# Squared-ReLU attention and a maxout layer on one core: a fourth query step by seven products, with z of the second sequence turned earlier

## The chip, the core and the metric

The kernel runs on one core of a Trainium2 chip. Its engines work side by side: TensorE (PE in the profile, PEld its weight loads) multiplies, VectorE (DVE) and ScalarE (ACT) do the elementwise work, GpSimd (POOL) and SyncE (SP) issue transfers. The metric is the device time of one execution in microseconds. Three runs of the kernel before gave 937.58, 938.73 and 940.17 us: median 938.73.

## The reference

For each of 8 sequences of 3072 rows, with z of 64 columns and u and v of 256:

```
scores = (z @ z.T) / 3072
attn   = maximum(scores, 0) ** 2
x      = u * (attn @ v)                 # 24576 rows of 256
out    = maximum(x @ w1, x @ w2) @ w_out    # 1024 hidden columns
```

The attention matrix is symmetric, so a block that one step has computed can be transposed for a later one. The kernel uses max(x@w1, x@w2) = relu(x@(w1-w2)) + x@w2, so that x@w2@w_out becomes x@(w2@w_out), with w2@w_out (W2o) computed once.

## The kernel before, in words

**Steps.** A step n is one sequence b and 512 of its queries (s = 0 to 5): 48 steps. Its 3072 keys are 24 blocks of 128, in 6 groups of four. A *pair* (n, k0) is two key blocks against 512 queries. Its scores are two matmuls that fill one PSUM tile of the pool `mm` (three tiles for the whole kernel), a relu on ACT or DVE takes them to an `a_sb` tile in SBUF, and a square follows there. Steps 0 to 3 compute all 12 pairs themselves. From step 4 on a step takes most groups from earlier steps by DMA transposes (`aT`, issued on SP) and computes fewer pairs, its diagonal group among them.

**Product with v.** A *plain* step (n < PLAIN, here steps 0 to 3) multiplies 24 blocks by two halves of v: 48 matmuls of 512 columns. The other steps use a scheme of the Strassen kind: each group takes 14 matmuls of 256 columns (six X, eight Y) in place of what would be eight of 512. X of all groups comes first, then Y. In exchange DVE folds v (four subtractions per group and sequence, one of them in place, after the last plain read of that group), adds blocks of the attention tiles (`es`, three or four additions per group of 128x512; four `es` tiles), and puts the result together (`e`, `t`) before it is scaled by u to `xT`.

**Second part.** d(n), 16 matmuls with w1-w2 in four jobs, a relu each to `g_sb`; o(n), 40 matmuls with w_out and W2o in two jobs, two copies to `o_sb` and a store. They lag: a non-plain step n does o(n-3), then X, d(n-2), Y. Before, plain step 3 has d(0), W2o with o(0), and d(1) laid among its products, each after six more key blocks. W2o needs w_out loaded and w2 loaded and turned (`w2T_sb`).

**What sets the order.** The order on PE is written out by a planner (lines 888 to 1033). It lists the work without scores, with planned times (`begins`). Scores are put in by *windows* of three pairs (the first three windows have two), in order of step and key. Going backwards from the last window, each is put at the latest allowed spot that is not later than when its first reader needs it less a latency (6.5 us for a step's own pairs, or 2.592 us where n <= 3 is plain), and not later than the next window's spot less a gap (2.1 us for early windows, 2.4 us later). A spot is not allowed inside d, o or W2o (`shared`), nor within 0.86 us behind or 1.7 us ahead of one, and in steps before step 3 only every 2.592 us from the step's start (`apart`). I call these early spots *slots*: four in each of steps 0, 1 and 2, slot 0 to slot 11. A window for which no spot is left goes to the very start of the list:

```python
found = [i for i in spots if begins[i] <= limit]
i = found[-1] if found else 0
laid.setdefault(i, []).insert(0, w)
limit = begins[i] - (GAP if w > n_first else GAP_FIRST)
```

Windows 0 and 1 are done in a hand-written head, and window 2 is always put behind the first two product jobs (lines 1019 and 1020). By the rule, window 14 (pairs 6, 8, 10 of step 3) has slot 11, each window before it one slot less, and window 3 (pairs 12, 14, 16 of step 0) slot 0; windows 15 to 18 stand within step 3.

All other engines follow a list scheduler (lines 1279 to 1332): with a cost for each job it repeatedly takes, over all engines, the job that can start first, and among those that can start at the same moment the one that is due first. DVE leaves a relu to ACT where ACT would end it sooner. The result is a fixed program order on each engine.

**Loads and turns.** `at_step(b, s, us)` names the first PE job at or behind that planned time after the start of a step. The load of z for sequence 1 (POOL, into `z_sb`) comes at step 3 plus 5 us, its two turns into `zT` (SP, DMA transposes) at step 4 plus 4 us; w_out is loaded at step 2 plus 9 us. The first score window of sequence 1 (window 19) stands early in Y of step 4.

Of the kernel before, what the change touches and what calls it, by code (L numbers as in the profile page):

```python
# [11 lines left out]
def kernel(  # L12
# [36 lines left out]
    LAG = 3  # L49
    NDIR = 3  # L50
    NDIAG = 3
    PLAIN = 4
    NA, NT = 12, 12
    scale = 1.0 / S
    c2 = float(scale * scale)
# [30 lines left out]
    def load(timed=False, **kw):  # L86
        dma = pin(nc.gpsimd.dma_start(**kw))
        if timed:
            tc.add_manual_dep(
                dma.ins,  # L90
                newest[0].name,
                mybir.DependencyInfo(mybir.DependencyClass.Sync, mybir.DependencyReason.DATA),
                reason="timed load",
            )
# [40 lines left out]
    w_out_sb = consts.tile([P, KF, D], bf16)  # L135
# [39 lines left out]
    def job(key, ways, fn, deps=(), new=None, uses=(), after=(), lag=100):  # L175
        assert key not in jobs, key
        jobs[key] = Job(key, ways, fn, deps, new, uses, after, lag)
# [5 lines left out]
    def tile_of(pool, key):  # L183
        return bufs[pool, key].tile

    class Step:
        def __init__(self, n, b, s):
            self.n, self.b, self.s, self.q = n, b, s, seqs[b]
            self.plain = n < PLAIN
            self.count = [0] * KD  # L190
# [74 lines left out]
    def add_v(b, g, at):  # L265
        buf("v", (b, g), lambda: vpool.tile([P, G, D], bf16, name="v_sb"))

        def fetch(_):
            load(
                timed=at is not None,  # L270
                out=tile_of("v", (b, g)),
                in_=v[b].rearrange("(p t) d -> p t d", p=P)[:, ds(g * G, G), :],
            )

        job(("v", b, g), {"POOL": 1300}, fetch, new=("v", (b, g)), after=at or (), lag=8000)
# [184 lines left out]
    def add_sums(st, g):  # L460
        n = st.n
        es = ("es", (n, g))
        buf("es", (n, g), lambda: spool.tile([P, 3, GW], bf16, name="es"))
        if g in st.early:
            src = ("T", (st.b, g, st.s))
            i = NG * st.b + g
            ready = [("turn", i, k0) for k0 in (G * st.s, G * st.s + 2)]
        elif g == st.s:
            src = ("A", (n, g))
            ready = [("square", n, None), ("square", n, -1), ("turn", n, None, 0), ("turn", n, None, 1)]  # L470
        else:
            src = ("A", (n, g))
            ready = [("square", n, k0) for k0 in (G * g, G * g + 2)]
# [417 lines left out]
    def put(ns, shares, key, reads=()):  # L891
        work.append((ns, shares, key, reads))

    def put_d(n):
        if n >= 0:
            for i in range(KF // 2):
                put(864, True, ("d", n, i))

    def put_o(n, per=2):
        if n >= 0:  # L900
            for i in range(G // per):
                put(1090 * per, True, ("o", n, i))

    def rows_read(st, g):
        if g in st.early:
            return [((NG * st.b + g, k0), LAT_TURNED) for k0 in (G * st.s, G * st.s + 2)]
        if g == st.s:
            return [((st.n, None), LAT_DIAG)]
        return [((st.n, k0), LAT_OWN) for k0 in (G * g, G * g + 2)]

# [3 lines left out]

    for n, st in enumerate(steps):
        if not st.plain:
            put_o(n - LAG)
            for which in range(2):
                if which:
                    put_d(n - LAG + 1)  # L920
                for g in st.groups:
                    for m in range(G // 2):
                        put(
                            PE256 * (4 if which else 3),
                            False,
                            ("XY"[which], n, g, m),
                            rows_read(st, g) if not which else (),
                        )
            continue
        within = {}  # L930
        lat = LAT_OWN if n > LAG else 6 * 432
        if n == LAG:
            within = {
                3: lambda: put_d(0),
                6: lambda: (put(1800, True, ("w2o",)), put_o(0)),
                9: lambda: put_d(1),
            }
        own = st.rows
        n_plain = 0

        def put_plain(ks, dcs, reads):
            global_i = len(plain_todo)
            i = sum(t[0] is st for t in plain_todo)
            plain_todo.append((st, i, ks, dcs))
            put(PE512 * len(ks) * len(dcs), False, ("plain", st.n, i), reads)

        for i, k0 in enumerate(own):
            if i in within:
                within[i]()
            if i in ((0, 1) if n else ()) + (len(own) - 2, len(own) - 1):  # L950
                if i in (0, len(own) - 2):
                    ks = [own[i], own[i] + 1, own[i + 1], own[i + 1] + 1]
                    for dc in range(KD):
                        put_plain(ks, [dc], [((n, own[i]), lat), ((n, own[i + 1]), lat)])
                continue
            for k in (k0, k0 + 1):
                put_plain([k], range(KD), [((n, k0), lat)])
# [38 lines left out]

    for n in range(PLAIN, len(steps)):
        i = first_of[n]
# [13 lines left out]
    for w in reversed(range(len(windows))):  # L1012
        limit = min([limit] + [due[r] for r in windows[w] if r in due])
        found = [i for i in spots if begins[i] <= limit]
        i = found[-1] if found else 0
# [24 lines left out]
    def at_step(b, s, us):  # L1040
        return pe_job_at(starts[NG * b + s] + us * 1000)
# [32 lines left out]
    def add_z(b, at, turn_at):  # L1074
        def fetch(_):
            load(
                timed=True,
                out=z_sb_0[:, 1 : 1 + NSB, :],
                in_=z[b].rearrange("(p t) d -> p t d", p=P),
            )  # L1080

        def turn_z(_):
            seqs[b].zT = make_zT(z_sb_0)

        job(("z", b), {"POOL": 1800}, fetch, after=at, lag=7500)
        job(("zT", b), {"SP": 3500}, turn_z, deps=[("z", b)], after=turn_at, lag=3500)
# [9 lines left out]
            add_u(n, at_step(pb, ps, 2 if pb == 0 else 4))  # L1096
    for b in range(1, B):
        if b == 1:
            z_at, zT_at = (3, 5), (4, 4)
            v_at = [(4, 8), (4, 14), (5, 1), (5, 4), (5, 9.5), (5, 11)]  # L1100
        else:
            z_at, zT_at = (2, 9), (3, 12)
            v_at = [(3, 8), (4, 2), (4, 8), (4, 13), (5, 9.5), (5, 11)]
        add_z(b, at_step(b - 1, *z_at), at_step(b - 1, *zT_at))
        for g, at in zip([1, 2, 3, 4, 5, 0], v_at):
            add_v(b, g, at_step(b - 1, *at))
# [4 lines left out]
    for tile_sb, source, key, at, new, rows in (  # L1111
        (lambda: tile_of(*W2), moe_w2, "w2", (0, 7), W2, "(c p) f -> p c f"),
        (lambda: w1_sb, moe_w1, "w1", (1, 3), None, "(c p) f -> p c f"),
        (lambda: w_out_sb, moe_w_out, "wo", (2, 9), None, "(c p) d -> p c d"),
    ):

        def fetch(_, tile_sb=tile_sb, source=source, rows=rows):
            load(timed=True, out=tile_sb(), in_=source.rearrange(rows, p=P))

        job((key,), {"POOL": 2000}, fetch, new=new, after=at_step(0, *at), lag=6500)  # L1120
# [57 lines left out]
    for args in plain_todo:  # L1178
        st, i, ks, dcs = args
# [4 lines left out]
    for st in steps:  # L1184
        if not st.plain:
            for g in st.groups:
                add_sums(st, g)
        add_ends(st)
# [231 lines left out]
```

## Time and profile before

| | us |
|---|---|
| median of three runs | 938.73 (937.58 to 940.17) |
| the profiled execution, its own time | 938.97 |
| its span, first to last instruction | 937.2 |
| PE busy | 927.7 (99%) |
| DVE busy | 763.2 (81%) |
| ACT busy | 688.4 (73%) |
| POOL busy | 58.6 (6%) |

The span lies 1.77 us below the execution's time. The granted clock of TensorE is 1.00 over the whole span. In the timeline a line is a run of like instructions on one engine: start, duration, line of the code, operation, tiles, shape, count, and in brackets the idle time ahead of it with what ended it. Nearly all matmuls are recorded at line 80, a helper, and so the tile names tell them apart: `s_ps<-zT` are scores, `acc<-...` products with v, `s_ps<-xT,w_sb` is d, `s_ps<-w_out_sb,...` and `s_ps<-W2o_sb,xT` are o. L219 and L221 are relus on ACT and DVE, L225 and L227 squares. Recorded durations of matmuls overlap; the chain's lines give the pace.

### The profile page before, as it was taken

To read this page: it belongs to the slowest core of one execution; us is meant where nothing else is said; L and a number is where in the kernel's file an instruction comes from. 1 tells how busy PE (TensorE), PEld (TensorE's weight loads), DVE (VectorE), ACT (ScalarE), POOL (GpSimd) and SP (SyncE) were. 2 spreads that over 40 slices of the span, in tenths; PEclk is the share of its full clock that TensorE was granted. 3 is DMA by queue.
4 is the path that set the end of the run, shared out by engine and by line. 5 is a ranking of instruction groups with operands and counts; after the bars stand their busy time and mean duration, and the time that the engine had idled before them with its cause. 6 is when DMAs were issued, how large, how long until landed. Compare 5 with 4: busy or idle time off the path is not lost.

```text
span 937.2 us, 18895 instructions
## 1 busy us (share of the span) xinstructions
PE 927.7 (99%) x7318; PEld 667.4 (71%) x7326; DVE 763.2 (81%) x1890; ACT 688.4 (73%) x829; POOL 58.6 (6%) x115
## 2 busy tenths in 40 slices
PE   8999999999999999999999999999999999999998
PEld 3355677777777777777777777777767777777786
DVE  6963898878987889778897888888888887988751
ACT  7876786579856797677877778876787658885634
POOL 2000100000000000000000000000100000000000
PEclk9999999999999999999999999999999999999999
DMA  8996998998989888899998978998899798987611
GB/s 140 168 171 111 168 167 154 156 166 136 180 149 167 146 145 162 171 163 144 142 166 173 162 136 142 188 153 160 145 164 163 148 149 169 150 166 133 124 47 68
DMA packets 365866, 140.84 MB, mean 150 GB/s; under 512 B 344272, under 2 KB 345936, under 8 KB 365776
## 3 DMA queue, kind: packets, MB, share of 16 engines
q1 hardware_dynamic: 349216, 109.89, 62.9%
q0 software_dynamic: 16560, 29.74, 21.8%
q8 instruction: 57, 0.93, 0.4%
q14 instruction: 33, 0.27, 0.1%
HBM read 59.77 MB, written 25.17 MB: 91 GB/s over the span
## 4 chain that ended last, share of the span: by engine, by line
PE 96%; ACT 2%; DMA 1%; SPq 1%; DVE 0%; issue 0%
PE s_ps L80 48%; PE acc L80 48%; DMA zT<-z_sb 1%; ACT a_sb L219 1%; SPq L83 1%; ACT g_sb L219 0%; ACT a_sb L225 0%; DMA o_sb<-in_z_dram 0%; PE tpz L109 0%; DVE a_sb L221 0%; ACT zT L110 0%; DVE a_sb L227 0%; DVE xT L240 0%; ACT o_sb L230 0%; DVE z_sb L154 0%
## 5 line engine op out<-in xcount | busy, mean ns | idle before, releaser
L80 PEld LDWEIGHTS <-v_sb 128*128 128x128 bf16 x2304 | 223.8, 98 | 83.8 <-issue 38.0
L219 ACT ACTIVATE a_sb<-s_ps 128x1024 bf16<-128x1024 f32 (+1 forms) x236 | 217.1, 975 | 35.8 <-PE s_ps L80 33.0
L225 ACT ACTIVATE a_sb<-a_sb 128x1024 bf16<-128x1024 bf16 (+1 forms) x224 | 218.5, 1013 | 0.1
L80 PE MATMUL s_ps<-w_out_sb,g_sb 128*128 128x256 bf16 x1504 | 194.9, 273 | 0.0
L80 PE MATMUL acc<-es,v_sb 128*128 128x256 bf16 x844 | 192.9, 274 | 0.0
L219 ACT ACTIVATE g_sb<-s_ps 128x1024 bf16<-128x1024 f32 x181 | 170.8, 1028 | 12.2 <-PE s_ps L80 12.2
L80 PE MATMUL s_ps<-xT,w_sb 128*128 128x512 bf16 x768 | 173.4, 379 | 0.0
L80 PEld LDWEIGHTS <-lf 128*128 128x128 bf16 x1584 | 155.0, 98 | 21.6
L233 DVE TENSOR_TENSOR es<-a_sb 128x512 bf16<-128x512 bf16 x300 | 119.8, 422 | 59.8 <-PE acc L80 59.6
L80 PE MATMUL acc<-es,lf 128*128 128x256 bf16 x740 | 167.1, 273 | 0.0
L80 PE MATMUL acc<-a_sb,lf 128*128 128x256 bf16 x600 | 163.5, 273 | 0.0
L80 PEld LDWEIGHTS <-g_sb 128*128 128x128 bf16 x1504 | 147.1, 98 | 17.5
L80 PE MATMUL acc<-a_sb,v_sb 128*128 128x256 bf16 (+1 forms) x784 | 150.6, 298 | 0.9 <-issue 0.5
L221 DVE TENSOR_SCALAR a_sb<-s_ps 128x1024 bf16<-128x1024 f32 (+1 forms) x112 | 127.5, 1140 | 21.3 <-PE s_ps L80 20.9
L80 PE MATMUL acc<-aT,v_sb 128*128 128x256 bf16 x668 | 139.7, 273 | 0.0
L80 PEld LDWEIGHTS <-w_sb 128*128 128x128 bf16 x768 | 75.2, 98 | 81.0
L230 ACT COPY e<-acc 128x512 f32<-128x512 f32 x88 | 52.1, 592 | 105.5 <-PE acc L80 105.2
L230 ACT COPY o_sb<-s_ps 128x512 f32<-128x512 f32 (+1 forms) x92 | 53.2, 578 | 87.8 <-PE s_ps L80 87.8
L80 PE MATMUL s_ps<-zT 64*128 64x512 bf16 (+1 forms) x696 | 94.8, 366 | 4.0 <-DMA zT<-z_sb 2.9
L227 DVE TENSOR_TENSOR a_sb<-a_sb 128x1024 bf16<-128x1024 bf16 (+1 forms) x124 | 79.6, 652 | 0.1
L80 PE MATMUL s_ps<-W2o_sb,xT 128*128 128x256 bf16 x384 | 73.3, 273 | 0.0
L80 PE MATMUL acc<-aT,lf 128*128 128x256 bf16 x244 | 66.5, 273 | 0.0
(53 smaller groups left out, 701.9 us busy)
## 6 DMA issues: line engine op xcount, KB each, us to landing
out_dram<-o_sb SPq DMA_DIRECT2D x47, 512.0 KB, 3.8
v_sb<-in_v_dram POOLq DMA_DIRECT2D x48, 256.0 KB, 4.9
u_sb<-in_u_dram POOLq DMA_DIRECT2D x48, 256.0 KB, 5.3
aT<-a_sb SPq DMA_TRANSPOSE x228, 4.1
z_sb<-in_z_dram POOLq DMA_DIRECT2D x7, 384.0 KB, 5.2
a_sb<-a_sb SPq DMA_TRANSPOSE x88, 2.6
w_sb<-in_moe_w_dram POOLq DMA_DIRECT2D x2, 512.0 KB, 7.7
uT<-u_sb SPq DMA_TRANSPOSE x48, 3.3
```

The lines of the kernel that those rows point to most:

```text
L80: newest[0] = pin(nc.tensor.matmul(*args, **kw)).ins
L83: pin(nc.sync.dma_start(**kw))
L219: pin(nc.scalar.activation(out_ap, in_ap, AF.Relu))
L221: pin(nc.vector.tensor_single_scalar(out=out_ap, in_=in_ap, scalar=0.0, op=ALU.max))
L225: pin(nc.scalar.activation(ap, ap, AF.Square))
L227: pin(nc.vector.tensor_mul(ap, ap, ap))
L230: pin(nc.scalar.copy(out_ap, in_ap) if eng == "ACT" else nc.vector.tensor_copy(out_ap, in_ap))
L233: pin(nc.vector.tensor_add(*args))
```

## The change

Step 3 becomes a step of the seven-product scheme (PLAIN goes from 4 to 3). It still computes all 12 pairs itself, so that its groups are 0 to 5, all taken from its own tiles; the condition for the diagonal group asks for `st.diag` now, which step 3 does not have. Its order on PE is d(0), W2o, o(0), X, d(1), Y. Its pairs are due by the rule of the other non-plain steps (6.5 us ahead of X). The load of w_out moves to step 2 plus 2 us, that of z for sequence 1 to step 2 plus 11 us, and its turn to step 3 plus 8 us.

```diff
-    PLAIN = 4
+    PLAIN = 3
...
-        elif g == st.s:
+        elif st.diag and g == st.s:
             src = ("A", (n, g))
...
     def rows_read(st, g):
...
-        if g == st.s:
+        if st.diag and g == st.s:
             return [((st.n, None), LAT_DIAG)]
         return [((st.n, k0), LAT_OWN) for k0 in (G * g, G * g + 2)]
...
         if not st.plain:
+            if n == LAG:
+                put_d(0)
+                put(1800, True, ("w2o",))
             put_o(n - LAG)
...
-        within = {}
         lat = LAT_OWN if n > LAG else 6 * 432
-        if n == LAG:
-            within = {
-                3: lambda: put_d(0),
-                6: lambda: (put(1800, True, ("w2o",)), put_o(0)),
-                9: lambda: put_d(1),
-            }
...
         for i, k0 in enumerate(own):
-            if i in within:
-                within[i]()
...
-            z_at, zT_at = (3, 5), (4, 4)
+            z_at, zT_at = (2, 11), (3, 8)
...
-        (lambda: w_out_sb, moe_w_out, "wo", (2, 9), None, "(c p) d -> p c d"),
+        (lambda: w_out_sb, moe_w_out, "wo", (2, 2), None, "(c p) d -> p c d"),
```

`add_sums`, `add_ends` and the planner are unchanged otherwise; they now serve step 3 as they serve steps 4 to 47.

## The prediction

> **What bounds the kernel now.** I read the page's busy times first, then the chain that ended last, then who waited for whom, and then the timeline of the first 100 us, where the change lies. The page's first part:
>
> ```profile
> span 937.2 us, 18895 instructions
> PE 927.7 (99%) x7318; PEld 667.4 (71%) x7326; DVE 763.2 (81%) x1890; ACT 688.4 (73%) x829; POOL 58.6 (6%) x115
> ```
>
> PE is busy for all but 9.5 us, so a change can gain only by less PE work or by removing one of PE's few waits. The list of waits (total, times, longest) has one large one on PE:
>
> ```profile
> PE s_ps L80 <- DMA zT<-z_sb: 2.9, 1, 2.9
> ```
>
> The chain shows what it hangs on, two turns of z for sequence 1, and the pace of the work around it (start, length, count):
>
> ```profile
> 57.14 3.45 PE s_ps L80 x16
> ...
> 60.60 0.86 PE acc L80 x4
> ...
> 64.09 6.11 PE s_ps L80 x56
> ...
> 87.77 8.18 DMA zT<-z_sb
> ...
> 145.36 3.93 PE acc L80 x36
> ```
>
> The pace: d takes 3.45 us, W2o with o(0) 6.11, a plain product 0.86/4 = 0.215, a product of 256 columns 3.93/36 = 0.109. The wait itself in PE's timeline, and PE's start, where the change will also act:
>
> ```profile
> 10.12 0.61 PE L80 MATMUL s_ps<-zT 64*128 64x512 bf16 x4 [0.32 <-DVE zT L110]
> 11.23 0.39 PE L80 MATMUL s_ps<-zT 64*128 64x512 bf16 x2 [0.51 <-ACT a_sb L219]
> 11.79 0.81 PE L80 MATMUL acc<-a_sb,v_sb 128*128 128x512 bf16 x3 [0.16 <-issue]
> ...
> 15.39 0.82 PE L80 MATMUL s_ps<-zT 64*128 64x512 bf16 x6
> 16.15 2.76 PE L80 MATMUL acc<-a_sb,v_sb 128*128 128x512 bf16 x12
> ...
> 95.99 0.71 PE L80 MATMUL s_ps<-zT 64*128 64x512 bf16 x6 [2.87 <-DMA zT<-z_sb]
> ```
>
> Window 3 at 10.12 and 11.23 (slot 0), its third pair waiting for a relu to free PSUM; window 4 at 15.39 (slot 1), the next one is at 18.84 and so on, 3.45 us from slot to slot, of which 0.76 are the window (15.39 to 16.15). ACT and DVE at the start:
>
> ```profile
> 11.22 1.06 ACT L225 ACTIVATE a_sb<-a_sb 128x1024 bf16<-128x1024 bf16 x1
> 12.18 1.00 ACT L219 ACTIVATE a_sb<-s_ps 128x1024 bf16<-128x1024 f32 x1
> 13.08 1.05 ACT L225 ACTIVATE a_sb<-a_sb 128x1024 bf16<-128x1024 bf16 x1
> 14.03 1.01 ACT L219 ACTIVATE a_sb<-s_ps 128x1024 bf16<-128x1024 f32 x1
> ...
> 11.18 2.35 DVE L221 TENSOR_SCALAR a_sb<-s_ps 128x1024 bf16<-128x1024 f32 x2
> 13.45 0.68 DVE L227 TENSOR_TENSOR a_sb<-a_sb 128x1024 bf16<-128x1024 bf16 x1
> 14.05 1.22 DVE L221 TENSOR_SCALAR a_sb<-s_ps 128x1024 bf16<-128x1024 f32 x1
> ```
>
> Both run without a pause: a relu every 0.90 us on ACT and 1.15 on DVE, squares 0.95 and 0.60.
>
> **Seven products in step 3.** Out: 48 x 0.215 = 10.32 us. In: 84 x 0.109 = 9.16. **Gain 1.16**, all on PE. DVE gets 24 additions, back to back 0.34 each (DVE's timeline has five of them from 98.56 to 99.90), 8.2 us, plus seven small operations and four scalings of 0.42 for two of 0.69; ACT two copies of 0.59. From 60 to 90 us DVE is busy only 3.07, 5.18 and 2.42 of each 10 us, so I cost them at nothing; without that cover the last two groups' sums (2.7 us), which wait for an `es` tile until Y has begun, would stop PE. Steps 4 and 5 lose one addition each.
>
> **z turned earlier.** The load now issues in d(0), about as early as before (then 61.13), but the turns come behind o(0) instead of after o(1), some 19 us sooner (67.4 for 86.42, by the sum below). With 8.2 us to land they are there about 17 us ahead of window 19. **Gain 2.87.** Next late at that place: nothing, the `mm` tiles are free and later windows ran unhindered. On SP the two turns take 4.66 us; queued behind them are the store of o(0), turns of step 3 (first read in X of step 4) and of its diagonal. The load of z passes that of u(4) on POOL (0.53 us of issue), which nobody needs for 20 us. w_out issues at about 47 for 53.71 on POOL; its landing took 7.0, and W2o asks for it at 61.
>
> **Small waits around step 3.** Products at 50.87 and 62.42 start 0.16 us late each, and the first ones of step 3 wait 0.07 for xT(2) at 53.46. Behind step 2 now comes d(0), which needs neither. Between 0 and 0.4, I take a **gain of 0.3**.
>
> **o(0) directly behind W2o and d(0).** Four relus of d(0) ended 4.83 us after d(0) began (56.98 to 61.81); o(0) will ask for them at 3.45 + 1.75 = 5.2. A square in ACT's way costs up to 0.95, less the 0.4 of slack. Between 0 and 0.6; I take a **loss of 0.2**.
>
> **The score windows.** This is the part that the diff does not show. X of step 3 reads its first pairs 9.6 planned us after the step's start, one group each 0.65 us, so with the 6.5 us of latency all four windows of step 3 are due between 3.1 and 5.7 us into it: inside d(0), W2o and o(0), where no spot is. Window 16 falls back to slot 11, and so every earlier one moves two slots forward: window 5 gets slot 0, and windows 4 and 3 find none and go to the start of the list with it. So nine pairs, not three, are scored ahead of the first product, through three PSUM tiles. Walking the scheduler's rule by hand (a square that can start goes before a relu that becomes ready 0.2 us later; the same walk on the old order gives the rows above), ACT does square, relu, square, relu, relu, square, relu; DVE relu, relu, square, relu, relu, square, relu. With the pitches above the relus free PSUM at 12.4, 13.1, 13.5 (window 3) and 15.0, 15.3, 15.9 (window 4), so the last pair of window 5 is scored at 16.0 and the first product starts at 16.3 instead of 11.8. Window 2 then waits for a relu until 17.9, eight products follow, and slot 1 comes at 19.95 instead of 15.39: 4.56 later. Two windows of 0.76 have been done ahead, and are missing in step 3 later: **loss 4.56 - 1.52 = 3.04**. Lower bound: all relus ahead of all squares gives slot 1 at 18.5, a loss of 1.5. Upper: one more square of 0.95 on each engine in the way, 5. The walk is nearest to the rows, so I take 3.04. After it, slots of 3.45 us follow as before: three relus and squares take 2.8 us of ACT and 2.4 of DVE.
>
> **Sum.** -1.16 - 2.87 - 0.3 + 0.2 + 3.04 = -1.1 us on the profiled execution's 938.97, which stands 0.24 over the median: 937.6 against 938.73. With all bounds: 935.8 to 940.3.
>
> **Rivals.** *The start costs little* (relus first, or the squares' place in the order kinder): loss 0 to 1.4, time 934.6 to 936.0. For it: ACT and DVE have 3 us of squares to spare there. Against it: the rule by which the old order comes out right.
>
> *The clock falls at the start.* At 1.19 six matmuls of 512 columns take 2.74 us, 0.45 each, and full pace is only there after 7: 5.5 us at half speed. If the thin scores between 10 and 16 us brought that back, it would cost 2 to 2.7 us: 939.6 to 940.3. Against it: behind the 2.87 us of waiting the next 24 products took 2.73, full pace. [...]
>
> *W2o waits for the turned w2* (the slower end). Before, its turn was issued at 45.03 and landed 6.1 us later, with W2o at 63.93: slack of 9 to 13 us. By the sum, the issue comes at about 49.5 to 52 (its trigger is 4.56 later, behind turns of 2 us each in a DMA stretch with a share of 1.08), landing 55.6 to 58, and W2o stands at 57.9 + 3.45 = 61.3. Should the queue hold it beyond 61.3, each us is one on PE, in order; from 65.4 on the kernel is over 0.3% slower, 941.6 to 943.6. For it: four turns took 10.77 us on SP at 57.79. Against it: slack is still 3 us.
>
> **Numbers.** Three tenths of a per cent, 2.8 us, is about what measuring this kernel tells from no change: 935.9 to 941.5 is "same". Forecast 0.56, cheap start 0.22, clock 0.10, w2 0.12. Faster: 0.22 and the forecast's lower edge, 0.03. Slower: 0.12 and 0.02 for edges. The range 934.9 to 941.2 leaves out the w2 case and the cheapest starts, under 2 in 10.
>
> **What would show it.** First product near 16.3 and slot 1 near 20.0; pairs of `s_ps<-zT` at 12 to 16 us each waiting on relus. No wait on `zT`; turns of z at 67 to 76. Step 3's part: d, W2o, o, 36 products, d, 48 products without a pause, and o(1) near 81.6 (before 80.33). Wrong would be: a first product by 13, a wait ahead of W2o or Y, or matmuls of 512 columns at 0.45 after 10 us.

## The result, and the profile after

Over 18 runs each, the changed kernel takes 940.47 us (median, 938.21 to 943.68), the kernel before 938.00 (935.50 to 940.17). The ratio is 1.0026 [1.0015, 1.0037]: slower by 2.4 us, between 1.4 and 3.5. The forecast was 1.1 us faster, so its sign was wrong and it stands 3.5 us off, though the time lies inside its range and within the 0.3% that it called no change.

The profiled execution of the changed kernel took 939.5 us. The page's first part:

```profile
span 937.7 us, 19013 instructions
PE 929.6 (99%) x7362; PEld 671.2 (72%) x7362; DVE 770.6 (82%) x1919; ACT 689.8 (74%) x833; POOL 58.4 (6%) x115
```

PE has 1.9 us more busy time than before (929.6 against 927.7), although 48 matmuls of 512 columns have been traded for 84 of 256, which was to save 1.16. In all PE waits less than before (8.1 us of the span against 9.5); some matmuls last longer. PE's timeline shows which:

```profile
9.33 0.61 PE L80 MATMUL s_ps<-zT 64*128 64x512 bf16 x4 [0.32 <-DVE zT L110]
10.45 0.39 PE L80 MATMUL s_ps<-zT 64*128 64x512 bf16 x2 [0.51 <-ACT a_sb L219]
11.66 0.61 PE L80 MATMUL s_ps<-zT 64*128 64x512 bf16 x2 [0.83 <-DVE a_sb L221]
12.45 1.03 PE L80 MATMUL s_ps<-zT 64*128 64x512 bf16 x4 [0.17 <-ACT a_sb L219]
14.30 1.52 PE L80 MATMUL s_ps<-zT 64*128 64x512 bf16 x6 [0.82 <-ACT a_sb L219]
15.76 1.89 PE L80 MATMUL acc<-a_sb,v_sb 128*128 128x512 bf16 x4
...
20.35 0.82 PE L80 MATMUL s_ps<-zT 64*128 64x512 bf16 x6
```

Four products of 512 columns last 1.89 us at 15.76, where four took 1.03 before (at 60.43); two scores take 0.61 at 11.66 and 0.39 at 10.45. I read the same stretch in windows of 3.41 us, half of the 6.83 us that the clock stays at 1.00 and then at 0.50 in this trace (columns: the window, its length, PE busy with the count of matmuls, granted clock, DMA share, GB/s):

```profile
4.78:8.19 3.41, 3.41 (x34) 1.00 1.10 170
8.19:11.61 3.42, 1.82 (x10) 1.00 1.12 202
11.61:15.02 3.41, 2.36 (x10) 0.50 0.94 175
15.02:18.43 3.41, 3.41 (x12) 0.50 0.31 61
18.43:21.84 3.41, 3.41 (x20) 1.00 1.00 190
```

The clock stands at half from 11.61 to 18.43 us. Before, the stretch from 9.73 to 13.14 had PE busy for 2.20 of 3.41 us and the clock at 1.00. Later in the same timeline:

```profile
58.21 3.62 PE L80 MATMUL s_ps<-xT,w_sb 128*128 128x512 bf16 x16
61.66 1.91 PE L80 MATMUL s_ps<-w_out_sb,w2T_sb 128*128 128x256 bf16 x16
...
81.59 0.27 PE L80 MATMUL acc<-es,v_sb 128*128 128x256 bf16 x1 [0.40 <-DVE es L233]
...
95.18 0.86 PE L80 MATMUL s_ps<-zT 64*128 64x512 bf16 x6
```

The 2.87 us of waiting for z at window 19 are gone. W2o follows d(0) without a pause. One new wait has come, 0.40 us for an `es` tile near the end of Y of step 3.

To set executions side by side I measure from window 3 (9.33 here, 10.12 before), because the stretch ahead of it takes 9.2 to 10.3 us in the 14 profiles. From there slot 1 comes after 11.02 us (before 5.27), and d(3) after 101.03 (before 100.91).

### The profile page after: what moved, and what is told of

Same layout as the page of the kernel before. It is cut to its first block, busy times and chain, and to the rows that moved or that the text cites. A ratio compares the mean times of both kernels' runs of the same rounds, so it can differ in the third digit from the quotient of the medians.

```text
span 937.7 us, 19013 instructions
## 1 busy us (share of the span) xinstructions
PE 929.6 (99%) x7362; PEld 671.2 (72%) x7362; DVE 770.6 (82%) x1919; ACT 689.8 (74%) x833; POOL 58.4 (6%) x115
## 4 chain that ended last, share of the span: by engine, by line
PE 96%; DMA 1%; DVE 1%; ACT 1%; SPq 0%; issue 0%; DVEq 0%
PE s_ps L80 48%; PE acc L80 48%; DMA uT<-u_sb 1%; ACT a_sb L219 0%; DVE es L233 0%; DMA o_sb<-in_z_dram 0%; ACT a_sb L225 0%; SPq L83 0%; PE tpz L109 0%; DVE a_sb L221 0%; DVE a_sb L233 0%; ACT zT L110 0%; ACT o_sb L230 0%; DVE lf L236 0%; DVE a_sb L227 0%
## 5 line engine op out<-in xcount | busy, mean ns | idle before, releaser
L80 PE MATMUL acc<-es,v_sb 128*128 128x256 bf16 x864 | 197.8, 274 | 1.0 <-DVE es L233 0.9
L80 PEld LDWEIGHTS <-lf 128*128 128x128 bf16 x1620 | 158.5, 98 | 23.7 <-issue 1.1
L233 DVE TENSOR_TENSOR es<-a_sb 128x512 bf16<-128x512 bf16 x312 | 125.3, 425 | 60.7 <-PE acc L80 60.7
L80 PE MATMUL acc<-es,lf 128*128 128x256 bf16 x756 | 170.8, 273 | 0.0
L80 PE MATMUL acc<-a_sb,lf 128*128 128x256 bf16 x624 | 170.1, 273 | 0.0
L80 PE MATMUL acc<-a_sb,v_sb 128*128 128x256 bf16 (+1 forms) x768 | 144.9, 294 | 0.0
L233 DVE TENSOR_TENSOR a_sb<-a_sb 128x512 bf16<-128x512 bf16 x156 | 66.3, 426 | 1.1
```

Of the source, the lines that this page charges most:

```text
L80: newest[0] = pin(nc.tensor.matmul(*args, **kw)).ins
L233: pin(nc.vector.tensor_add(*args))
```

## The experiments

The theory after the result: the start costs the 3.04 us of waits that the prediction worked out, and on top of it the clock falls; step 3 and z bring what was forecast. The main rival: the clock only shows up beside the loss, and the loss is the waits alone, or a wait in step 3.

In the table, "slot 1" and "d(3)" are counted from window 3 in the profiled execution; slot 1 is left out where the slots lie otherwise. Ratios are to the kernel before, run beside each.

| kernel | median us (runs) | ratio | slot 1 | d(3) |
|---|---|---|---|---|
| before | 938.00 (18) | 1 | 5.27 | 100.91 |
| after | 940.47 (18) | 1.0026 [1.0015, 1.0037] | 11.02 | 101.03 |
| blank products at the start | 938.71 (12) | 1.0008 [0.9994, 1.0021] | 9.90 | 101.62 |
| z alone | 936.15 (12) | 0.9975 [0.9963, 0.9988] | 5.27 | 98.12 |
| z alone, again | 936.71 (12) | 0.9978 [0.9965, 0.9991] | 5.27 | 98.12 |
| windows alone | 943.25 (6) | 1.0049 [1.0031, 1.0068] | 11.13 | 104.13 |
| without the z move | 945.83 (5) | 1.0082 [1.0065, 1.0098] | 11.28 | 107.22 |
| six pairs ahead | 938.43 (12) | 1.0014 [0.9989, 1.0039] | | 99.76 |
| relus first | 946.49 (6) | 1.0071 [1.0048, 1.0095] | 10.29 | 108.00 |
| windows spread | 936.64 (12) | 0.9974 [0.9960, 0.9988] | | 97.93 |
| windows spread, again | 936.74 (12) | 0.9990 [0.9967, 1.0012] | | 97.41 |
| spread, two waits taken out | 936.96 (12) | 0.9975 [0.9961, 0.9988] | | 96.85 |
| w_out earlier | 938.55 (1) | | 11.05 | 101.06 |
| spread, w_out earlier | 936.92 (12) | 0.9982 [0.9964, 1.0000] | | 97.40 |

### Blank products at the start

The changed kernel; PE gets products of a blank tile behind each of the first nine score pairs, so that it is busy while it waits for PSUM. Nothing reads them.

```diff
             for j in range(2):
                 score(q, s_tile(key)[:, j, :], j, k0 + j, st.s, 0, G)
+            if ("score", n, k0) in front:
+                idle((0, 2, 3, 2, 0, 4, 0, 1, 0)[front.index(("score", n, k0))])
...
+    front = pe_order[: pe_order.index(("plain", 0, 0))]
```

> The changed kernel with 13 products of a blank tile (512 columns, result discarded) put between the first nine score pairs on PE, so that TensorE is not thin between 10 and 16 us; nothing else changes. Theory F (the front: nine pairs ahead of the first product cost PE 3.0 us of waits, and the fall of the granted clock to 0.5 from 11.6 to 18.4 us costs another 1.2 to 1.7): the clock stays at 1.00 from about 5 us on, slot 1 comes about 1.2 us sooner than in the changed kernel (20.35), time 938.7 to 939.4. Rival L (the front is made up for later, and the loss sits in the later program, in waits for the sums and for u): the clock may stay, the time does not move: 940.2 to 940.8.

The windows of this kernel at the same place, and its W2o:

```profile
9.73:13.14 3.41, 3.05 (x15) 1.00 1.11 205
13.14:16.56 3.42, 3.27 (x18) 1.00 0.43 80
```

```profile
62.65 1.92 PE L80 MATMUL s_ps<-w_out_sb,w2T_sb 128*128 128x256 bf16 x16 [1.25 <-ACT g_sb L219]
```

With PE busy for 3.05 and 3.27 us of these windows the clock stays at 1.00, and slot 1 comes 9.90 us after window 3. The prediction's walk had 9.83 at full clock. So the waits were sized right, and the fall costs 11.02 - 9.90 = 1.1 us at this place. In the medians the two kernels differ by 0.0018, 1.7 us, with intervals that would also take 0.1 or 3. The profiled execution gives its gain back at W2o, which waits 1.25 us. The view names ACT for it, but the relus of d(0) were through: the weight loads of `w2T_sb` stood 1.7 us for the DMA of that tile, which landed 12.5 us after its issue, at 62.6. So the clock is not all that the forecast missed: with it held, the kernel stands 0.75 us over the kernel before by the medians (between 0.6 under and 2.0 over), where 1.1 under was forecast.

### z alone

The kernel before with only the load and turn of z moved.

```diff
-            z_at, zT_at = (3, 5), (4, 4)
+            z_at, zT_at = (2, 11), (3, 8)
```

> The kernel before with only z of sequence 1 loaded at step 2 plus 11 us and turned at step 3 plus 8 us; step 3 stays plain. Theory F: the 2.87 us of waiting ahead of the first window of sequence 1 go, nothing else moves: 2.9 us below the kernel before, about 935.1. Rival L (another wait takes its place, in later steps): 0 to 1 us below, 937 to 938.

Window 19 in PE's timeline, with no wait:

```profile
96.01 0.82 PE L80 MATMUL s_ps<-zT 64*128 64x512 bf16 x6
```

From window 3 to d(3) it gains 100.91 - 98.12 = 2.79 us, the wait almost to the last. The medians give 2.35 [1.1, 3.5] here and, in a second series, 2.06 [0.8, 3.3]; 2.87 lies within both.

> The kernel of the run named z_only once more (plain step 3, z early): 2.1 to 2.4 us under the kernel before, as measured. Both theories.

### Windows alone

The kernel before, with its product of step 3 as it was, but windows 3 to 16 put where the changed kernel has them.

```diff
+    at_of = {w: i for i, ws in laid.items() for w in ws}
+    slots = [at_of[w] for w in range(3, 15)]
+    laid = {i: [w for w in ws if w > 16 or w < 3] for i, ws in laid.items()}
+    for w in range(16, 2, -1):
+        laid.setdefault(slots[max(w - 5, 0)], []).insert(0, w)
```

> The kernel before (step 3 plain, z where it was) with windows 3 to 16 put where the changed kernel has them: window 16 at slot 11, each earlier one a slot less, and windows 3, 4 and 5 at the very start. Theory F: 3.0 us of waits on PE in the first 20 us and the fall of the clock (1.2 to 1.7 us), less 0.3 for the two windows that no longer interrupt step 3; the wait for zT stays 2.9: about 4 us over the kernel before, 941.5 to 942.5. Rival L: under 1.5 us over it, below 939.5.

It is 0.49% slower, the loss without the gains, and 0.75 us above its expectation. Slot 1 comes 11.13 us after window 3, and the clock is at half from 12.12 to 18.95. At d(3) it is 3.22 us behind the kernel before; its wait for z was 1.79 instead of 2.87, so that the start cost 3.22 + 1.08 = 4.3 us. That is the 3.04 of the prediction and 1.2 of clock. Step 3 of this kernel has no seven-product scheme, so the loss comes from the windows and not from step 3's arithmetic.

### Without the z move

The changed kernel with z loaded and turned where it was before.

```diff
-            z_at, zT_at = (2, 11), (3, 8)
+            z_at, zT_at = (3, 5), (4, 4)
```

> The changed kernel with z loaded and turned where it was before (step 3 plus 5 us, step 4 plus 4 us). Theory F: the wait for zT ahead of window 19 is back, 2 to 2.9 us: 942.5 to 943.3, 4.5 to 5.3 over the kernel before. Rival L (the wait was hidden or is replaced): 940 to 941.5.

It came out over both expectations. PE's wait for z, and the windows around it:

```profile
99.36 1.25 PE L80 MATMUL s_ps<-zT 64*128 64x512 bf16 x6 [3.37 <-DMA zT<-z_sb]
```

```profile
94.64:98.05 3.41, 1.35 (x11) 1.00 1.00 135
98.05:101.47 3.42, 2.11 (x11) 0.50 0.96 282
101.47:104.88 3.41, 3.41 (x18) 0.50 0.11 24
```

Behind the wait of 3.37 us the clock is at half a second time, from 98.05 to 104.88. In the changed kernel the stretch from d(2) to d(3) is 19.60 us, here 25.53: 3.37 of the difference is the wait, and 2.56 is left for the matmuls at half clock behind it.

This is what misled the prediction. In the profiled execution before, the wait of 2.87 us fell across two windows, with PE busy for 1.47 and 2.49 us, and the clock stayed at 1.00:

```profile
91.65:95.06 3.41, 1.47 (x11) 1.00 1.05 251
95.06:98.48 3.42, 2.49 (x23) 1.00 0.86 126
```

Other executions of the kernel before had a lower clock: of 92 beside the experiments, 17 show a mean clock of 0.998 or less, and in the largest series the five at 0.998 have a median of 940.40 against 938.14 of those at 1.00. Of 24 runs with z alone, none is below 0.999. That the wait for z is what takes the clock down in those 17 is argued from this, not seen: the one profile of the kernel before has no fall.

### Six pairs ahead

The changed kernel with slots every 2.16 planned us instead of 2.592, so that two more windows find one, and six pairs instead of nine are scored ahead of the first product.

```diff
-        return n >= LAG or (at - starts[n]) % (6 * 432) == 0
+        return n >= LAG or (at - starts[n]) % (5 * 432) == 0
```

> The changed kernel with early windows allowed each 2.16 us of a step (five slots a step): one window more than before stands at the front (six pairs ahead of the first product), not two. Theory F: waits at the front cost 1.2 us instead of 3.0; the granted clock either holds (936.9) or falls as with nine pairs (938.7). Rival P: no gain over the changed kernel, 940 or more.

```profile
10.43:13.85 3.42, 1.70 (x12) 1.00 1.11 205
13.85:17.26 3.41, 3.08 (x10) 0.50 0.15 28
```

Here the clock is at half for one window of 3.41 us, 13.85 to 17.26, where the changed kernel has two; PE was busy for 3.08 us of it, and full pace followed. The median fits the expectation with a fall (938.7), but by itself it decides little: the six runs at 0.998 have a median of 938.15, the three at 1.00 of 937.86, and two runs of 946.75 and 949.53 widen the interval.

### Relus first

The changed kernel, with the squares of the first nine pairs held behind the last of their relus: the prediction's lower bound for the start.

```diff
+    front = pe_order[: pe_order.index(("plain", 0, 0))]
...
+    for key in front:
+        jobs[("square",) + key[1:]].after.append(("relu",) + front[-1][1:])
```

> The changed kernel with the squares of the first nine pairs held behind the last of their relus, so that ACT and DVE free PSUM first; nine pairs still stand ahead of the first product. Theory F: front waits 1.5 us instead of 3.0, slot 1 about 1.5 us sooner; with the clock falling as before 939.0, with the clock holding 937.3. Rival (the squares are needed as soon, and PE waits for them ahead of its first products of step 0 instead): 940 to 941.

Later, on DVE and on PE:

```profile
48.59 1.29 DVE L240 SCALAR_TENSOR_TENSOR xT<-acc,uT 128x512 bf16<-128x512 f32 x2 [5.17 <-DMA uT<-u_sb]
49.34 1.01 PE L80 MATMUL acc<-a_sb,v_sb 128*128 128x512 bf16 x2 [4.86 <-DVE xT L240]
```

It missed. Slot 1 comes 10.29 us after window 3, sooner than 11.02 and with one window of half clock (14.13 to 17.55). But a later product waits 4.86 us until DVE has done `xT`, and DVE had itself waited 5.17 us for u's turn. The clock falls again from 48.27 to 55.09. Why that turn came so late is not shown. The kernel says nothing on the cheap start, only that its price can't be had by this edit.

### Windows spread

The changed kernel with a spot allowed every 0.432 planned us in steps 0 to 2. The gap of 2.1 then sets the distance: 14 windows stand 2.16 planned us apart, and two pairs are scored ahead of the first product.

```diff
-        return n >= LAG or (at - starts[n]) % (6 * 432) == 0
+        return n >= LAG or (at - starts[n]) % 432 == 0
...
-    laid.setdefault(spots[0] + 2, []).insert(0, 2)
+    laid.setdefault(spots[0], []).insert(0, 2)
```

> The changed kernel, but the planner may put early score windows at any key block (not only each 2.592 us) and window 2 goes ahead of the first products: the 14 windows ahead of d(0) then stand every 2.16 planned us, two pairs are scored ahead of the first product and not nine, all four windows of step 3 stay ahead of d(0). Theory F (front waits 3.0, clock 1.8): both go, the clock stays at 1.00; what is left is z (2.1 to 2.9), the products (1.2) and small waits (0.3) as gains, sums and W2o (0.4 to 1) as losses: 934.5 to 935.7, about 3 under the kernel before. Rival P (pace: ACT and DVE cannot take three pairs in 2.9 us, so that the waits for relus only move into the slots of steps 0 to 2): 937 or more.

The pile at the start is gone, the clock is at least 0.999 in all 12 runs, and the kernel is faster than before by 0.26% [0.12, 0.40]. Against the changed kernel that is 0.0052, 4.9 us. It fell about 1 us short of its expectation. Two waits in step 3 were in its way, one for the `es` tile, the other at W2o:

```profile
58.75 1.92 PE L80 MATMUL s_ps<-w_out_sb,w2T_sb 128*128 128x256 bf16 x16 [0.47 <-DMA w2T_sb<-w_sb]
```

### Spread, with the two waits taken out

On top of it, w2 is turned one step sooner, and three relus that stood on DVE among the last sums of step 3 go to ACT.

```diff
-        after=at_step(0, 2, 2),
+        after=at_step(0, 1, 6),
...
+    for key in (("relu", 4, 22), ("relu", 5, None), ("relu", 5, -1)):
+        jobs[key].ways = {"ACT": jobs[key].ways["ACT"]}
```

> The kernel of the run named spread (seven products, z early, windows every 2.16 us) with the turn of w2 at step 1 plus 6 us instead of step 2 plus 2, and the three relus of window 18 left to ACT. Theory W (what the seven products save in step 3, 1.2 us, goes to two new waits there: 0.47 us and more ahead of W2o, 0.4 to 0.56 us for the last sums in Y): both waits go from the profile and the time is about 1 us under that of spread. Rival (the gain is lost elsewhere, in the windows' closer pace or in later sequences): the waits go, the time stays within 0.4 us of spread.

> The kernel of the run named spread once more, beside spread_fix and z_only2 on one chip: 2.3 us under the kernel before, as measured. Theory W: it stands level with z_only2 within 0.5 us, since its 1.2 us of saved products are spent on the two waits in step 3. Rival (the seven products are a gain by themselves once the front is mended): 1 us under z_only2.

Both waits went from step 3. The second series of the spread kernel has two runs with a lower mean clock (940.87 at 0.998, 945.31 at 0.995), which widen its interval; its other ten have a median of 936.03. The profiled executions of this kernel and of z alone (second series) have window 3 at 10.26 and 10.27. d(3) of this kernel and of z alone:

```profile
107.11 3.62 PE L80 MATMUL s_ps<-xT,w_sb 128*128 128x512 bf16 x16
```

```profile
108.39 3.62 PE L80 MATMUL s_ps<-xT,w_sb 128*128 128x512 bf16 x16
```

This kernel is ahead by 1.28 us, where the trade of products was to give 1.16. The medians do not show it: 936.96, 936.74 and 936.71 for this kernel, the spread one and z alone, with intervals of about 1.2 us to each side. The rival had forecast this (the waits go, the time stays); theory W's 1 us is not borne out, though the intervals do not exclude it. Between the three I can't choose.

### w_out earlier

In the changed kernel w2's turn took 11.9 us from issue to landing (before 6.1), with the load of w_out issued at 48.32, just ahead of it at 48.54. Two kernels move that load ahead, one from the changed kernel and one from the spread one.

```diff
-        (lambda: w_out_sb, moe_w_out, "wo", (2, 2), None, "(c p) d -> p c d"),
+        (lambda: w_out_sb, moe_w_out, "wo", (1, 10), None, "(c p) d -> p c d"),
```

> The changed kernel with the load of w_out issued at the second step plus 10 us (about 38 us in) instead of at the third plus 2 us (48.3 us), where it went out 0.2 us ahead of w2's turn. Theory (the load of w_out, 512 KB, is what slows the turn): w2's turn lands some 6 to 8 us after its issue at about 48.5, as it took 6.1 before, and W2o at about 61.7 has 5 us of slack. Rival (that stretch of the transfers is slow whatever is loaded in it): it lands 10 to 12 us after its issue as now, slack about 1 us. The start is as in the changed kernel by both: the clock falls at about 12 and slot 1 comes 11.0 us after window 3. Time about 939.5 to 941 by both, since the profiled execution of the changed kernel had no wait there.

> The kernel with the windows spread at the start (clock held, two pairs ahead of the first product), with the load of w_out moved in the same way and nothing else. Theory: w2's turn lands 6 to 8 us after its issue at about 47 (11.4 and 10.7 in the two runs of the spread kernel), W2o at about 58.3 never waits for it, and the time is at or up to 0.5 us below that of the spread kernel, 0.9965 to 0.998 of before. Rival: the turn still takes 10 to 12 us and W2o waits in some executions; time as the spread kernel's, 0.9974 to 0.999. The wait of 0.40 us for the sums of the last groups stays by both.

SP's timeline in the changed kernel, and in this one:

```profile
46.25 2.19 SPq L83 DMA_TRANSPOSE uT<-u_sb  x1
48.54 4.67 SPq L83 DMA_TRANSPOSE w2T_sb<-w_sb  x1
```

```profile
47.16 5.33 SPq L83 DMA_TRANSPOSE uT<-u_sb  x1
52.58 5.89 SPq L83 DMA_TRANSPOSE w2T_sb<-w_sb  x1
```

The edit was weaker than its expectation has it: step 1 plus 10 us is only some 2.4 planned us ahead of step 2 plus 2, since a step has 10.4, and the load went out at 45.25 instead of 48.32. The turn now lands in 8.4 us, but it is issued 4.0 us later, because u's turn ahead of it on SP takes 5.33 us instead of 2.19. It is there at 61.0, with W2o at 61.72: the slack has not grown. In the spread kernel it landed in 7.4 us, at 56.3, against 58.7 and 57.0 without the edit, and the time is the spread kernel's. With the load moved, w2's turn itself was quicker (8.4 us for 11.9), but the turn ahead of it was slower (5.33 for 2.19), and nothing was gained. What makes the transfers slow there is not settled; the load some 10 us ahead, as the expectation had meant it, was not tried.

## Why the prediction was wrong, by its own steps

**The score windows: right.** Which window goes where, and the order on ACT and DVE at the start, came out as walked by hand. DVE of the changed kernel reads relu, relu, square, relu, relu, square, relu:

```profile
10.39 2.35 DVE L221 TENSOR_SCALAR a_sb<-s_ps 128x1024 bf16<-128x1024 f32 x2
12.66 0.68 DVE L227 TENSOR_TENSOR a_sb<-a_sb 128x1024 bf16<-128x1024 bf16 x1
13.26 1.22 DVE L221 TENSOR_SCALAR a_sb<-s_ps 128x1024 bf16<-128x1024 f32 x1
14.95 1.23 DVE L221 TENSOR_SCALAR a_sb<-s_ps 128x1024 bf16<-128x1024 f32 x1 [0.48 <-PE s_ps L80]
16.09 0.68 DVE L227 TENSOR_TENSOR a_sb<-a_sb 128x1024 bf16<-128x1024 bf16 x1
16.69 1.22 DVE L221 TENSOR_SCALAR a_sb<-s_ps 128x1024 bf16<-128x1024 f32 x1
```

At full clock (blank products) slot 1 comes 9.90 us after window 3, for 9.83 predicted. The loss of 3.04 stands.

**"The clock falls at the start": this is the step that failed.** It was a rival with a chance of 0.10, and by the mean clock it came true in all 18 runs, one of which was profiled: five have a mean clock of 0.998, eleven 0.996, two less. 0.996 is what 6.83 us at half clock make of 937.7, 0.998 what 3.41 us make. The prediction's own sign of it, matmuls of 512 columns at 0.45 us after 10 us, stands at 15.76. Its price was put at 2 to 2.7 us. In the profile it is 1.1 to 1.2 (11.02 against 9.90 with blank products, against 9.83 by the walk); I take it that part of the slow matmuls stood in for waits. The runs at 0.996 are 2.0 us above those at 0.998 (medians 940.94 and 938.94). The fall takes away the 1.1 us of gain that was forecast. That the kernel came out slower, and not level, it does not explain (the sum, below).

The argument against it was that full pace held after 2.87 us of waiting. That was one execution, in which the wait straddled two windows, with PE busy for 1.47 and 2.49 us of 3.41. The prediction went by the longest idle time, and that does not sort these profiles: at the start of the changed kernel no single gap of PE was over 0.83 us, and the clock fell, behind a window with PE busy for 1.82 of 3.42 us. In the six profiles with a fall at the start the window ahead of it had PE busy for 1.57 to 1.82 us, about half, with the idle time in several short waits. Whether the busy time or the series of waits decides is not shown.

**z turned earlier: right.** No wait, turns issued at 66.9 and 68.4 (67.4 predicted), landed 5.6 us on. The gain shows at d(3) as 2.79 for 2.87.

**Seven products in step 3: right in the gain, wrong in "I cost them at nothing".** In the changed kernel slot 1 to o(1) went from 64.94 to 62.11 us, 2.83 less. Of that 1.52 are the two windows done ahead and 1.16 the products; 0.40 was given back at the `es` wait, and 0.55 is left for the small waits and o(0) together, where the prediction had 0.3 less 0.2. The cover was there on average: DVE was busy for only 3.22 and 4.91 us of the two stretches of 10 us from 60 to 80. But the busy share of a stretch said nothing on the order. Ahead of the last group's sum stood a square and window 18's relu, which ran from 79.99 to 81.2.

**o(0) directly behind W2o and d(0): cost nothing.** No wait shows there. The 0.2 was within its bounds.

**"W2o waits for the turned w2": did not decide, but its margin was mis-sized.** The turn was issued at 48.5 (49.5 to 52 predicted) and landed at 60.4, not 55.6 to 58, because landing took 11.9 us where the row before had 6.1. The slack was 1.2 us instead of 3. In two other kernels it was used up, for 0.47 and 1.25 us.

**The sum.** In the profiled executions, from window 3 to d(3): -1.1 forecast, +1.2 for the clock, +0.4 for the `es` wait, about -0.45 for the small waits; that makes +0.05, and the traces show 101.03 - 100.91 = +0.12. Up to there the account closes. The medians say +2.4 [1.4, 3.5], so more than 1 us lies elsewhere. From d(3) to the end of the span the changed kernel takes 827.4 us and the kernel before 826.1. The difference lies in four steps, each the fifth of a later sequence: 0.74 us in the largest, 0.23, 0.16 and 0.08 in the others. In the largest PE waits 0.55 us for a sum, and DVE, in its program order, had waited 3.16 us for u's turn; DVE and PE in the changed kernel:

```profile
551.09 0.43 DVE L240 SCALAR_TENSOR_TENSOR xT<-t,uT 128x256 bf16<-128x256 f32 x1 [3.16 <-DMA uT<-u_sb]
555.77 0.27 PE L80 MATMUL acc<-es,v_sb 128*128 128x256 bf16 x1 [0.55 <-DVE es L233]
```

Before, that wait was 1.17 us. It varies: z alone has it in its second series at another sequence, 3.17 us, and the time behind d(3) is 826.1 to 828.1 in four profiles with the plain step 3, 826.4 to 829.2 in ten with the seven products. The means, 827.0 and 828.0, could differ. The kernel with the two waits taken out points the same way: at d(3) it is 100.91 - 96.85 = 4.06 us ahead of the kernel before, by its median only 2.35 (z alone: 2.79 at d(3), 2.06 and 2.35 by the medians). But with this scatter I leave open whether the change has a cost there, or whether it is in executions where w2's turn came too late.

## What to carry to other kernels

Before a step is made cheaper, look at what was planned around it: here the plain step 3 held the spots and the late due times for the score windows, and without it they piled up at the start, for 3.04 us of waits and 1.1 to 2 us of clock, more than the products and z brought. The series of short waits on PSUM cost twice here, as waits and as clock; either spread the work, which kept the mean clock at 0.999 or more in 45 of 48 runs and brought 4.9 us, or fill the gaps with products that nobody reads, which kept it in 11 of 12 and brought 1.7 us, between 0.1 and 3. And cover on an engine with a fixed program order is read from what stands ahead of the instruction that is waited for, not from the busy share: here DVE was busy for 4.91 us of the 10 from 70 to 80, and at 81.59 PE still waited 0.40 us for a sum.

## What the runs showed of the hardware

The clock records begin with full pace, at 4.78 us in the changed kernel and 6.32 in the kernel before; ahead of that six products of 512 columns take 2.74 us in both. From there to 925 us of the span all the stretches at half clock in twelve of the profiles last 3.41 or 6.83 us. At the start they are 11.61 to 18.43 in the changed kernel, 11.79 to 18.61 (w_out earlier), 12.12 to 18.95 (windows alone), 12.72 to 19.55 (without the z move), 13.85 to 17.26 (six pairs ahead) and 14.13 to 17.55 (relus first); later ones are 98.05 to 104.88 without the z move and 48.27 to 55.09 with relus first. The two falls without the z move lie 85.33 us apart, 25 times 3.413.

I read the same twelve profiles in windows of 3.41 us from the start of each one's clock records, as far. Each of the eight falls followed a window with PE busy for 1.82 us or less (1.82, 1.76, 1.75, 1.70, 1.63, 1.57, 1.35 and none), and no window with 2.02 or more was followed by one. Two windows between did not fall: 1.47 (before, at 91.65) and 1.81 (windows spread, again, at 322). So in these profiles a fall came only behind a window that was busy for 1.82 of 3.41 us or less, and such a window did not always bring one. What else decides, no run tried. Windows at half clock with 2.1 to 2.4 us busy were followed by a second one at half; the two with 3.08 were followed by full pace.

In all 18 runs of the changed kernel the mean clock is 0.998 or less. Its stretch of thin scores, from 9.9 to 15.8 us, is 5.9 us long, so that a window of 3.41 us lies within it for at least 2.9 us wherever the windows begin (an estimate from the two lengths). With six pairs ahead, where the stretch goes from 10.9 to 14.7, three of 12 runs kept the clock.
